# An FFT mixing layer and a hardswish MLP: the last inverse-transform stage packed into even and odd parts, mirrored output rows sent through a scratch tensor, and another ending of the last block

## The chip, the core and the metric

The kernel runs on one NeuronCore of a Trainium2 chip. TensorE (PE) multiplies matrices; its weight loads are shown as PEld. VectorE (DVE), ScalarE (ACT) and GpSimd (POOL) do elementwise work, and SyncE (SP) mostly issues DMAs. Each engine runs its own queue in order and waits for the others through semaphores. The metric is the device time of one execution in microseconds (us); the program's time is the median of several executions.

## The reference

```python
batch, seq, dim = (8, 3008, 256)          # n_freq = 1505, d_ff = 2048
X = np.fft.rfft(x, axis=1)
Y = X * (filt_r + 1j * filt_i)[None, :, :]
y = np.fft.irfft(Y, n=x.shape[1], axis=1).astype(np.float32)
h = y.reshape(24064, 256) @ w_in          # 256 x 2048
g = h * np.clip(h + 3.0, 0.0, 6.0) / 6.0
out = (g @ w_out).astype(np.float32)      # 2048 x 256
```

Everything is float32. The two weight matrices arrive as 64-bit floats and are turned into 32-bit ones by bit operations on DVE in the first microseconds of the kernel.

## The kernel before

**The transform.** A sequence of 3008 is written as 47 x 64 (token n = a * 64 + c). For each batch, `a_unit` (L391) transforms over a, storing 24 frequency rows k of real and imaginary parts in the DRAM tensor `z_tmp`; `b_unit` (L438, L447) transforms over c, `f_unit` and `y_unit` multiply by the filter, `bi_unit` (L482) transforms back over c and `g_store` (L499, L502) writes `g_tmp`. The last stage is `n_unit` (L535), which goes from 24 frequencies k back to 47 values of a, for each of 32 columns j. Column j of the transform gives two sets of 47 tokens, those of c = j and of the mirrored c = 64 - j. `t4_load` (L525 for batch 0, L528 for the others) brings five columns at a time, a chunk, from `g_tmp` to the tile `t4` with four DMAs, one column in each slot: rows 0-23 and 32-55 hold real and imaginary parts of c = j, rows 64-87 and 96-119 those of 64 - j. For each half dh of the 256 channels and each column, one matmul takes 128 rows x 128 channels of `t4` as its weights and streams the 94 columns of `wai[:, j]` (2 x 47 tokens); ACT copies the 470 results to `xn` (L541), channels on partitions and tokens along the row. `xn` is a ring of three blocks of 512 tokens. A float32 matmul shows in the profile as two passes, each a weight load and a matmul, so `n_unit` makes 20 passes for a chunk and half.

**The MLP.** 47 blocks of 512 tokens go through 8 steps p of 256 hidden columns each. Both products are done with a seven-multiplication scheme on 2 x 2 blocks (Strassen-Winograd). `t_sums` (L574) forms four sums of `xn` on POOL. `up_1` to `up_5` (L581) do seven 256-column matmuls into two PSUM tiles `al` and `be`; between them ACT and DVE copy partial sums out (L592, L593, L602, L607, L612, L621), and a later product into `al` may start only when the copy before it is done. `relu` (L626) and `hswish` (L631) give `g`; `g_sums` (L638-641) makes the sums for the down product, `down` (L657) does fourteen 128-column matmuls, and `out_1` to `out_5` (L693-716) add the seven results together into `o`. Block 0 alone is done without that scheme (`plain_up` L668, `plain_down` L679). `w_sums` (L308) turns the converted weights into the scheme's sums on POOL in steps 6 to 13.

**The order of work** is written out by hand. Step i of the main loop does the up product of (k, p) and the down product of the step before; `plan` holds, for each step, the units of the transform of the coming batch that are put after `up_1` (`do(True)`: matmul units) or at the end of the step (`do(False)`: the rest). The plan of `n_unit` is in `N_AT` and `N_FIRST`, and `t4_load` of a chunk is issued one chunk ahead, or for a batch's first chunk three steps ahead.

**The output.** `store` (L734) writes a finished block to `out` with one DMA for each run of up to 47 tokens within 128 partitions, 15 of them on average, all on SP's queue. After the last step, five DVE adds finish block 46 and its stores go out in runs of at most 32 rows over three queues.

Of the kernel before, what the change touches and what calls it, by code (L numbers as in the profile page):

```python
# [26 lines left out]
N = 3008  # L27
# [7 lines left out]
B = 8  # L35
# [16 lines left out]
RING = 3 * BLK  # L52
ND = (NJ + 1) * TOK


def outer(j, h):

    return (NC - j if j else HC) if h else j


def _make_tables():
# [3 lines left out]
    wai = np.zeros((P, HC, TOK))  # L65
# [26 lines left out]
    for q in range(64):  # L92
# [3 lines left out]
        wi[q, 3], wi[HALF + q, 3] = ab, sign * ab  # L96

        at = g % 2 * 32 + (q // 2 if q < 32 else 16 + (q - 32) // 2)
        wi[at, 0], wi[HALF + at, 0] = ab, sign * ab
# [11 lines left out]
        wi[q, 1], wi[HALF + q, 1] = ab, -ab  # L111
        wi[q, 2], wi[HALF + q, 2] = sign * ab, sign * ab
    start[:, :P] = np.eye(P)
    for j in range(HC):
        for h in range(2):
            to = slice(h * NA, (h + 1) * NA)
            for k in range(KH):
                m = 2.0 if k else 1.0
                th = 2 * np.pi * ((a * k * NC + outer(j, h) * k) % N) / N
                cs, sn = m * np.cos(th), m * np.sin(th)  # L120
                s = -1.0 if h else 1.0
                if j:
                    wai[k, j, to], wai[32 + k, j, to] = cs, -sn
                    wai[64 + k, j, to], wai[96 + k, j, to] = -s * sn, -s * cs
                else:
                    wai[h * 64 + k, j, to], wai[h * 64 + 32 + k, j, to] = cs, -sn
    direct = np.zeros((P, TC, ND))
    n = np.array([i * NC + outer(j, h) for j in range(NJ + 1) for h in range(2) for i in range(NA)])
    for k in range(KH - TC, KH):
        for q in range(64):  # L130
            th = 2 * np.pi * (((k + NA * q if q < 32 else NA * (q - 31) - k) * n) % N) / N
            direct[q, k - KH + TC], direct[HALF + q, k - KH + TC] = 2 / N * np.cos(th), -2 / N * np.sin(th)
    f = np.float32
    return wa.astype(f), (wai / N).astype(f), wb.astype(f), wi.astype(f), wf.astype(f), start.astype(f), direct.astype(f)
# [3 lines left out]
def kernel(  # L138
# [22 lines left out]
    g0_d = nc.dram_tensor("g0_tmp", (NC, 2, KH, D), FP32, kind="Internal").ap()  # L161
    g_d = nc.dram_tensor("g_tmp", (B, NU, 2, 2, NC, D), FP32, kind="Internal").ap()
# [22 lines left out]
    wai = const.tile([P, HC, TOK], FP32, name="wai")  # L185
# [3 lines left out]
    t4 = const.tile([P, 2 * NJ, D], FP32, name="t4")  # L189
    xn = const.tile([P, 2, RING], FP32, name="xn")  # L190
    w_all = const.tile([P, NP, 2, 7, P], FP32, name="w_all")
    w_in, w_out = ([w_all[:, p, i, :, :] for p in range(NP)] for i in range(2))
    half_c = const.tile([P, 1], FP32, name="half_c")
# [61 lines left out]
    def w_load(i, q):  # L255
        if W_AT[i] == "g":
            t = gp.tile([P, 7, 256], FP32, name="g")
            st["rest"] = t[:, 4:7, :].rearrange("p a n -> p (a n)")
            t = t.bitcast(I32)[:, 0:4, :].rearrange("p a n -> p (a n)")
        elif W_AT[i] == "x":  # L260
            t = xtp.tile([P, 4, 256], FP32, name="xt").bitcast(I32).rearrange("p a n -> p (a n)")
        else:
            t = op.tile([P, 1024], I32, name="bits", tag="o")
        q.dma_start(t.rearrange("p (a d) -> p a d", a=2), w_part(i)[0])
        st["bits", i] = t
# [39 lines left out]
    def w_sums(i, late):  # L305
        w = (w_in, w_out)[i % 2][i // 2]
        for o, x0, x1, op_ in (IN_SUMS, OUT_SUMS)[i % 2][3 * late:3 + late]:
            nc.gpsimd.tensor_tensor(out=w[:, o, :], in0=w[:, x0, :], in1=w[:, x1, :], op=op_)  # L308

# [9 lines left out]
    A11, S3, A12, A22, S1, S2, S4 = range(7)  # L319
    IN_SUMS = ((4, 1, 3, ALU.add), (5, 4, 0, ALU.subtract), (6, 2, 5, ALU.subtract), (1, 0, 1, ALU.subtract))  # L320
# [24 lines left out]
    def zt(dh):  # L345
        return (xn.rearrange("p a n -> p (a n)"), xs.rearrange("p i j d -> p (i j d)"))[dh]
# [141 lines left out]
    def g0_first(i):  # L488
        t = st["t3", 0, i]
        for v in range(2):  # L490
            for h in range(2):
                (nc.scalar, nc.sync)[v].dma_start(g0_d[ds(h * HC, NJ + 1), :, ds(2 * (i + v), 2), :].rearrange("c ri u d -> c ri (u d)"),
                                    t[ds(v * 64 + h * HC, NJ + 1)].rearrange("p ri u d -> p ri (u d)"))

    def g_store(b, i):
        t = st.pop(("t3", b, i))
        for v in range(2):
            if b == 0:
                nc.gpsimd.dma_start(g0_d[:, :, ds(2 * (i + v), 2), :].rearrange("c ri u d -> c ri (u d)"),  # L499
                                    t[ts(v, 64)].rearrange("p ri u d -> p ri (u d)"))  # L500
                continue
            nc.gpsimd.dma_start(g_d[b, i + v].rearrange("ri u c d -> c (ri u) d"), t[ts(v, 64)].rearrange("p ri u d -> p (ri u) d"))  # L502
# [3 lines left out]
    chunks = []  # L506
    for b in range(B):
        j = 0
        while j < HC:
            n = 1 if b == 0 and j == NJ else min(NJ, HC - j)  # L510
            chunks.append((b, j, n))
            j += n

    def token(i):
        b, j, n = chunks[i]
        return b * N + j * TOK, n * TOK

    def t4_load(i, k0=0, k1=KH, more=0):
        b, j, n = chunks[i]
        n += more  # L520
        for h in range(2):
            for ri in range(2):
                p0 = h * 64 + ri * 32
                if b == 0:
                    nc.sync.dma_start(t4[p0 + k0:p0 + k1, ds(i % 2 * NJ, n), :],  # L525
# [509 lines left out]
```

## Time and profile before

| | us |
|---|---|
| median of 3 runs | 2694.93 (2693.86 to 2696.06) |
| the profiled execution | 2693.65 |
| its span, first to last instruction | 2691.9 |

Mean granted TensorE clock: 0.998 of full speed.

| stretch of the span, us | PE busy | PEld busy | DVE | ACT | POOL | share of the DMA engines |
|---|---|---|---|---|---|---|
| 0 to 64, batch 0's transform | 57.55 | 40.57 | 48.24 | 25.45 | 15.62 | 0.88 |
| 64 to 128, block 0 | 62.61 | 38.59 | 58.89 | 26.51 | 8.89 | 0.79 |
| 128 to 170 | 41.34 | 36.52 | 25.78 | 20.18 | 31.53 | 0.49 |
| 694 to 1028, one batch in the middle | 334.00 | 297.12 | 254.38 | 164.80 | 44.86 | 0.24 |
| 2366 to 2676, no transform left but the last chunks | 310.00 | 292.61 | 204.03 | 153.45 | 18.74 | 0.06 |
| 2676 to 2692, the end | 3.89 | 3.51 | 4.96 | 1.35 | 4.11 | 0.12 |

Busy time is a union over the instructions of an engine. PE is busy without a gap from about 170 us to 2676 us; what it does there adds up to the time. [...]what one pass costs in a stream is the distance from start to start.

### The profile page before, as it was taken

The page shows a single profiled execution, that of the slowest core. Times are in us where ns is not written, and L with a number is a line of the kernel's source. Part 1 is how long each engine was busy: PE and PEld are TensorE (multiplying, and loading weights), DVE is VectorE, ACT ScalarE, POOL GpSimd, SP SyncE. Part 2 cuts the span into 40 slices and gives each one's busy share as a digit, 9 for nine tenths or more (in the row PEclk, how much of TensorE's full clock was granted, in tenths as well). Part 3 has the DMA queues.
Part 4 walks back from the last instruction along what each step waited for, and adds up shares of the span by engine and source line. Part 5 has one row for each costly group of instructions (what it writes and reads, how often), then busy time and mean ns, then how long its engine had stood idle before and what let it go on. Part 6 is the DMA issues. An engine that isn't in the chain of part 4 may idle for free.

```text
span 2691.9 us, 48842 instructions
## 1 busy us (share of the span) xinstructions
PE 2670.5 (99%) x18836; PEld 2364.3 (88%) x18836; DVE 2022.3 (75%) x3505; ACT 1306.9 (49%) x2612; POOL 369.4 (14%) x598
## 2 busy tenths in 40 slices
PE   9999999999999999999999999999999999999998
PEld 6688888888888889888898888888888898899997
DVE  7878867877678776787767777677876878766665
ACT  3444444545445454454544545445444454545443
POOL 2241021011210112101121101211012111000000
PEclk9999999999999999999999999999999999999999
DMA  8732233112331113311133212331123321110000
GB/s 254 213 90 66 53 97 98 55 37 54 90 96 55 38 53 89 96 55 39 53 89 96 56 40 55 89 93 56 39 57 90 93 62 31 42 31 18 18 9 17
DMA packets 106333, 185.95 MB, mean 69 GB/s; under 512 B 23333, under 2 KB 66021, under 8 KB 105781
## 3 DMA queue, kind: packets, MB, share of 16 engines
q1 hardware_dynamic: 88343, 138.12, 18.3%
q0 software_dynamic: 17152, 44.22, 6.2%
q8 instruction: 149, 2.44, 0.4%
q14 instruction: 83, 0.68, 0.1%
q10 hardware_dynamic: 606, 0.49, 0.1%
HBM read 110.80 MB, written 71.93 MB: 68 GB/s over the span
## 4 chain that ended last, share of the span: by engine, by line
PE 97%; DMA 1%; DVE 1%; ACT 0%; issue 0%; POOL 0%; SPq 0%; POOLq 0%; DVEq 0%; ACTq 0%
PE po L657 43%; PE al L581 24%; PE be L581 18%; PE psn L535 4%; PE psf L391 2%; PE psf L482 2%; PE psf L438 1%; PE po L679 1%; DMA g_tmp<-t 1%; PE al L668 0%; PE be L668 0%; DMA w_all<-in_x_dram 0%; PE psf L447 0%; PE po L447 0%; PE po L358 0%
## 5 line engine op out<-in xcount | busy, mean ns | idle before, releaser
L657 PEld LDWEIGHTS po<-w_all,g 128*128 128x128 f32 x10304 | 1363.2, 191 | 149.5 <-issue 41.4
L657 PE MATMUL po<-w_all,g 128*128 128x128 f32 x10304 | 1403.2, 276 | 0.6 <-DVE g L631 0.6
L626 ACT ACTIVATE r<-h,half_c 128x512 f32<-128x512 f32 x736 | 531.2, 722 | 329.6 <-DVE h L607 317.6
L631 DVE SCALAR_TENSOR_TENSOR g<-r,h 128x512 f32<-128x512 f32 x736 | 508.1, 690 | 205.3 <-ACT r L626 191.1
L581 PE MATMUL al<-xt,w_all 128*128 128x256 f32 x2208 | 660.1, 381 | 0.7 <-DVE h L612 0.6
L581 PE MATMUL be<-xn,w_all 128*128 128x256 f32 x1472 | 437.8, 379 | 0.0
L607 DVE TENSOR_TENSOR h<-be,s 128x512 f32<-128x512 f32 x368 | 254.3, 691 | 215.3 <-PE be L581 210.3
L581 PEld LDWEIGHTS al<-xt,w_all 128*128 128x128 f32 x2208 | 335.2, 192 | 2.1 <-DVE h L612 1.2
L581 PEld LDWEIGHTS be<-xn,w_all 128*128 128x128 f32 x1472 | 279.7, 190 | 37.9
L621 ACT ACTIVATE h<-al 128x256 f32<-128x256 f32 x368 | 141.3, 384 | 343.2 <-PE al L581 343.2
L612 DVE TENSOR_TENSOR h<-al,s 128x256 f32<-128x256 f32 x368 | 156.2, 425 | 165.8 <-PE al L581 164.8
L639 DVE TENSOR_TENSOR g<-g 128x512 f32<-128x512 f32 x368 | 256.2, 696 | 12.6
L602 ACT ACTIVATE s<-al 128x256 f32<-128x256 f32 x368 | 141.4, 384 | 205.9 <-PE al L581 203.8
L593 ACT ACTIVATE s<-be 128x256 f32<-128x256 f32 x368 | 141.4, 384 | 176.3 <-PE be L581 176.3
L581 PE MATMUL al<-xn,w_all 128*128 128x256 f32 x736 | 219.9, 381 | 0.5 <-ACT h L621 0.5
L581 PE MATMUL be<-xt,w_all 128*128 128x256 f32 x736 | 218.9, 379 | 0.0
L641 DVE TENSOR_TENSOR g<-g 128x256 f32<-128x256 f32 x368 | 170.1, 462 | 12.5
L592 ACT ACTIVATE s<-al 128x256 f32<-128x256 f32 x368 | 141.4, 384 | 70.3 <-PE al L581 70.3
L638 DVE TENSOR_TENSOR g<-g 128x256 f32<-128x256 f32 x368 | 157.3, 428 | 12.6
L581 PEld LDWEIGHTS be<-xt,w_all 128*128 128x128 f32 x736 | 139.8, 190 | 18.9
L412 POOL DMA_DIRECT2D z_tmp<-t x192 | 95.6, 505 | 417.3 <-DVE t L405 399.0
L502 POOL DMA_DIRECT2D g_tmp<-t x84 | 52.9, 634 | 581.9 <-ACT t L485 581.9
(144 smaller groups left out, 1810.2 us busy)
## 6 DMA issues: line engine op xcount, KB each, us to landing
g_tmp<-t POOLq DMA_DIRECT2D x96, 256.0 KB, 3.7
t<-g_tmp SPq DMA_DIRECT2D x188, 120.0 KB
t<-z_tmp SPq DMA_DIRECT2D x42, 512.0 KB
z_tmp<-t POOLq DMA_DIRECT2D x192, 96.0 KB, 3.3
out_dram<-o SPq DMA_DIRECT2D x321, 47.0 KB
xs<-in_x_dram SPq DMA_DIRECT2D x112, 128.0 KB
ft<-in_filt_r_dram SPq DMA_DIRECT2D x168, 64.0 KB
ft<-in_filt_i_dram SPq DMA_DIRECT2D x168, 64.0 KB
```

The source lines that it names most:

```text
L581: nc.tensor.matmul(ps, w_in[p][:, w, :], x, start=start, stop=stop, skip_group_check=True)
L592: nc.scalar.activation(out=s[:, 0, :], in_=al, func=AXT.Copy)
L593: nc.scalar.activation(out=s5, in_=be[:, 1, :], func=AXT.Copy)
L602: nc.scalar.activation(out=s[:, 1, :], in_=al, func=AXT.Copy)
L607: nc.vector.tensor_tensor(out=st["h"][0].rearrange("p (a n) -> p a n", a=2), in0=be, in1=s, op=ALU.add)
L612: nc.vector.tensor_tensor(out=st["h"][1][:, 256:512], in0=al, in1=s5, op=ALU.add)
L626: nc.scalar.activation(out=r, in_=st["h"][i], func=AXT.Relu, bias=half_c, scale=1.0 / 6.0)
L631: nc.vector.scalar_tensor_tensor(out=st["g", k, p][:, o:o + 2, :].rearrange("p a n -> p (a n)"), in0=st["r", i], scalar=1.0, in1=st["h"][i ...
L638: v.tensor_tensor(out=g[:, G1, :], in0=g[:, G3, :], in1=g[:, G22, :], op=ALU.add)
L639: v.tensor_tensor(out=g[:, G3:G2 + 1:2, :], in0=g[:, G3:G1 + 1, :], in1=g[:, G11:G11 + 1, :].broadcast_to([P, 2, 256]), op=ALU.subtract)
L641: v.tensor_tensor(out=g[:, G4, :], in0=g[:, G12, :], in1=g[:, G2, :], op=ALU.subtract)
L657: nc.tensor.matmul(st["po", k][bank][:, part, u, :], g[:, a, ts(u, P)], w_out[p][:, w, :], start=(p == 0 and n in OPENS and u == 0), stop= ...
```

## The change

**Even and odd parts.** For a real sequence, the tokens of c = j and their mirror images are C + S and C - S, where C comes from the real parts (cosines) and S from the imaginary parts (sines) of `g_tmp` alone. `bi_unit`'s table `wi` is changed so that its outputs are already these sums and differences. A column needs 48 rows for C and 48 for S. `t4_load` packs five columns' 240 rows into two weight tiles of 128 and 112 rows, for C and for S, and `n_unit` streams a table `groups` of 3 x 47 = 141 columns past each: four matmuls for a chunk and half in place of five. The third column's 48 rows lie partly in one tile and partly in the other, and both add into its 47 results. Columns left over (0 and 1, and seven columns of the last batch) are done one by one with 94 table columns and 96 rows. There are 46 full chunks and 20 single columns in the kernel, apart from the six columns that `direct` and `n_first` do at the start.

`xn` now holds C and S, 256 of each for a block, and the combination is moved into the sums of the MLP's scheme: `t_sums` makes seven POOL operations where there were four, and the weights' sums are others, with two of the seven scaled by 2 and -2 on ACT after POOL has made them.

**Stores.** Half 0 of a block's tokens goes to `out` directly, half 1 (the mirrored rows) to the DRAM scratch `o_tmp` in one DMA; when 16 columns are complete (15, 9, 10, 6 or part of one at the edges), one DMA from DRAM to DRAM copies them to their rows of `out`, backwards.

**The last block.** Its columns are arranged so that 7 DMAs write each half of it, its last down step is done without the seven-product scheme into two free PSUM tiles, and the outputs of the steps before it are added beside that. The column `b12` of the last weights, which the scheme overwrites, is saved and put back for this.

```diff
-RING = 3 * BLK
+PAIRS = BLK // 2
+RING = 3 * PAIRS
...
-    t4 = const.tile([P, 2 * NJ, D], FP32, name="t4")
-    xn = const.tile([P, 2, RING], FP32, name="xn")
+    t4 = const.tile([P, 8, D], FP32, name="t4")
+    xn = const.tile([P, 2, 2, RING], FP32, name="xn")
...
     def w_sums(i, late):
         w = (w_in, w_out)[i % 2][i // 2]
+        if late and i == 2 * NP - 1:
+            nc.scalar.activation(out=b12, in_=w[:, 1, :], func=AXT.Copy)
         for o, x0, x1, op_ in (IN_SUMS, OUT_SUMS)[i % 2][3 * late:3 + late]:
             nc.gpsimd.tensor_tensor(out=w[:, o, :], in0=w[:, x0, :], in1=w[:, x1, :], op=op_)
+        if late and i % 2 == 0:
+            for o, scale in ((S1, 2.0), (A22, -2.0)):
+                nc.scalar.activation(out=w[:, o, :], in_=w[:, o, :], func=AXT.Copy, scale=scale)
...
+    def t4_load(i):
...
+        both = t4[:, ds(s0, 4), :].rearrange("p (c s) d -> p s c d", c=2)
+        for q, j in enumerate(js):
+            for hh in range(2):
+                r, k = q * ATOM + hh * KH, 0
+                while k < KH:
+                    s_, p0 = divmod(r + k, P)
+                    m = min(KH - k, P - p0)
+                    nc.sync.dma_start(both[p0:p0 + m, s_, :, :],
+                                      g_d[b, hh * HC + j, :, k:k + m, :].rearrange("ri k d -> k ri d"))
+                    k += m
...
     def n_unit(i, dh):
         ps = psF.tile([P, 512], FP32, name="psn", tag="f")
-        for q in range(chunks[i][2]):
-            nc.tensor.matmul(ps[:, ts(q, TOK)], t4[:, i % 2 * NJ + q, ts(dh, P)], wai[:, chunks[i][1] + q, :], start=True, stop=True)
...
+        if len(js) == NJ:
+            for c in range(2):
+                for s_ in range(2):
+                    r = ROWS[s_]
+                    nc.tensor.matmul(ps[:, ds(c * NJ * NA + s_ * 2 * NA, SPAN)], t4[0:r, s0 + 2 * c + s_, ts(dh, P)],
+                                     groups[0:r, (js[-1] - 2) // NJ, s_, :], start=c == 0 and s_ == 0, stop=True,
+                                     skip_group_check=True)
+            pieces = [(0, n, o, ps[:, 0:2 * n])]
+        else:
+            for q, j in enumerate(js):
+                w = edges[0:2 * ATOM, FIRST.index(j), :] if i >= TAIL and j else ones[0:2 * ATOM, j, :]
+                nc.tensor.matmul(ps[:, ts(q, TOK)], t4[0:2 * ATOM, s0 + q, ts(dh, P)], w, start=True, stop=True)
...
     def t_sums(k):
-        for o, x0, x1 in ((0, b12, b11), (1, b22, t[:, 0, :]), (2, b22, b12), (3, b21, t[:, 1, :])):
-            nc.gpsimd.tensor_tensor(out=t[:, o, :], in0=x0, in1=x1, op=ALU.subtract)
+        for o, x0, x1, op_ in ((f1, c0, s0, ALU.subtract), (u, c0, c1, ALU.add), (v, s0, s1, ALU.add),
+                               (f4, u, v, ALU.subtract), (f5, u, v, ALU.add), (f2, c1, s1, ALU.add), (f3, f1, f2, ALU.add)):
+            nc.gpsimd.tensor_tensor(out=o, in0=x0, in1=x1, op=op_)
...
+    def last_down():
+        p, v, add = NP - 1, nc.vector.tensor_tensor, ALU.add
+        g, o = st["g", LAST, p], st["o", LAST][0]
+        hswish(LAST, p, 1)
+        ps = [psF.tile([P, 512], FP32, name="psf", tag="f") for t in range(2)]
+        for i, a in ((0, G11), (1, G12)):
+            for t in range(2):
+                for u in range(2):
+                    nc.tensor.matmul(ps[t][:, ts(u, D)], g[:, a + t, ts(u, P)],
+                                     w_out[p][:, 2 * i:2 * i + 2, :].rearrange("p j m -> p (j m)"),
+                                     start=i == 0 and u == 0, stop=i == 1, skip_group_check=True)
+        out_4(LAST)
+        v(out=o_at(LAST, 0, 1), in0=st["po", LAST][3][:, 1, :, :], in1=o_at(LAST, 0, 1), op=add)
+        for t, qs in ((0, (nc.sync, nc.gpsimd, nc.scalar)), (1, (nc.sync, nc.scalar))):
+            both = o[:, t, :, :].rearrange("p u d -> p (u d)")
+            v(out=both, in0=ps[t], in1=both, op=add)
+            store_last(t, qs)
...
+    def store(k):
+        o = st["o", k][0]
+        nc.sync.dma_start(o_d[ds(k * PAIRS, PAIRS)].rearrange("(u p) d -> p u d", p=P), o[:, 1, :, :])
+        for u, p, m, b_, j, a in runs(k):
+            for h in range(1 if j else 2):
+                nc.sync.dma_start(raw(out, b_ * N + row(j, h, a), [[NC * D, m], [1, D]]), o[p:p + m, h, u, :])
+        for b_, r, j, m, na in BACK.get(k, ()):
...
+            nc.sync.dma_start(bass.AP(tensor=out.tensor, offset=to, ap=a0),
+                              bass.AP(tensor=o_d.tensor, offset=o_d.offset + r * D, ap=a1))
+
+    def store_last(h, qs):
...
+        for n, (p, m, u, nu, to, du) in enumerate(parts):
+            ap = [[NC * D, m], [du, nu], [1, D]]
+            qs[n % len(qs)].dma_start(bass.AP(tensor=out.tensor, offset=out.offset + to, ap=ap), o[p:p + m, h, u:u + nu, :])
...
-            if up:
-                up_1(k, p)
+            if not up:
+                last_down()
+                break
+            up_1(k, p)
+            ends = k == LAST and p == NP - 1
...
-        v(out=o_at(k, 1, 1), in0=po[2][:, 0, :, :], in1=o_at(k, 1, 0), op=add)
-        v(out=o_at(k, 1, 0), in0=st["o", k][1][:, 1, :, :], in1=o_at(k, 1, 0), op=add)
-        store(k, 2, 4, qs)
-        v(out=o_at(k, 0, 1), in0=po[2][:, 0, :, :], in1=o_at(k, 0, 1), op=add)
-        v(out=o_at(k, 0, 1), in0=po[3][:, 1, :, :], in1=o_at(k, 0, 1), op=add)
-        store(k, 0, 2, qs)
```

In the step marked `ends`, `out_1`, `out_2` and `out_3` of block 46 run already beside the products of the step before the last. The last two chunks (`TO`) are written to `xn` in eight pieces for each half dh, because their tokens are laid out for `store_last`. The table for the first six columns is loaded at the start into a part of `wai` (564 columns, where eight columns' 752 were loaded before), the rest (1880 columns, before 2256) in step 0, and the first part again for the last batch near the end.

## The prediction

> **What bounds the kernel.** I read the page's busy times first, then the chain that ended last.
>
> ```profile
> PE 2670.5 (99%) x18836; PEld 2364.3 (88%) x18836; DVE 2022.3 (75%) x3505; ACT 1306.9 (49%) x2612; POOL 369.4 (14%) x598
> ...
> PE 97%; DMA 1%; DVE 1%; ACT 0%; issue 0%; POOL 0%; SPq 0%; POOLq 0%; DVEq 0%; ACTq 0%
> ```
>
> PE carries 97% of the chain. In the trace's waits, the rows in which PE waits for another engine add up to 3.2 us between 64 us and 2680 us. So a microsecond taken from PE's stream comes off the time, and what other engines gain or lose counts only where it makes PE wait, or after PE's last instruction.
>
> Next the price of one PE pass. The timeline of PE alone, around one `n_unit` with both halves (columns: start us, extent us, engine, line, form, count); a count in the last column divides the distance to the next start:
>
> ```profile
> 2023.32 0.59 PE L581 MATMUL be<-xt,w_all 128*128 128x256 f32 x2
> 2023.75 0.59 PE L581 MATMUL be<-xn,w_all 128*128 128x256 f32 x2
> 2024.18 2.37 PE L535 MATMUL psn<-wai,t 128*128 128x94 f32 x20
> 2026.38 0.64 PE L657 MATMUL po<-w_all,g 128*128 128x128 f32 x4
> ...
> 2027.72 1.05 PE L657 MATMUL po<-w_all,g 128*128 128x128 f32 x8
> 2028.62 0.38 PE L581 MATMUL al<-xt,w_all 128*128 128x256 f32 x1
> ```
>
> 256 columns: 0.43 / 2 = 0.215 us a pass. 128 columns: (2028.62 - 2027.72) / 8 = 0.1125. 94 columns: (2026.38 - 2024.18) / 20 = 0.110. From 256 to 128 columns the price halves; from 128 to 94 it hardly falls. Below 128 columns the pass is held by something that isn't the streamed columns, and each pass has its weight load beside it. This is where the change works: 94-column passes waste stream.
>
> **The last transform stage.** Before: the page counts 1000 passes at L535 (43, 24, 18% of the chain are the MLP, 4% this stage), 1000 x 0.110 = 110.0 us. After: 46 full chunks x 2 halves x 4 matmuls x 2 passes = 736 passes of 141 columns, and 20 single columns x 2 x 2 = 80 of 94 columns; the six first columns (24 passes elsewhere) don't change. No row has 141 columns. A straight line between 128 and 256 columns gives 0.1125 + 13/128 x 0.1025 = 0.123. The slope of the wide rows alone (the 512-column L668: four passes in 1.72 us in the chain, 0.43 each; 0.43 / 512 = 0.00084 a column) gives 0.118. I take 0.121, between them. 736 x 0.121 + 80 x 0.110 = 97.9, so **-12.1 us**; with 0.118 it is -14.4, with 0.123 -10.7. The early `plain_down` passes of 256 columns (L679) take 3.65 us for 16 in the chain, 0.228, 0.013 over the others; were the new passes to carry that too (0.136), -1.1 would be left. That is the outer end.
>
> A rule speaks against this. The Trainium skill (TensorE: Matmul & The Clock Gate, "Back-to-back issue gap") prices a pass by its columns, N / 2.4 + 2.5 ns, and Perfetto Trace Analysis ("Engine Utilization") halves the rate for float32, so about N / 1.2 + 2.5: 80.8 ns for 94 columns, 120 for 141. The stage would then go from 80.8 to 736 x 0.120 + 80 x 0.0808 = 94.8 us, 14 us dearer, because the change streams 111,296 columns where there were 94,000. The row decides: 110 ns, not 81, for 94 columns. The same page's "LDWEIGHTS" has 128 / 1.2 = 107 ns for loading 128 weight columns, whatever the rows, which fits the floor. For 141 columns the rule's 120 agrees with my 0.121.
>
> **The end.** Timeline from PE's last work to the last store:
>
> ```profile
> 2675.45 1.50 PE L657 MATMUL po<-w_all,g 128*128 128x128 f32 x12
> 2676.82 0.69 DVE L631 SCALAR_TENSOR_TENSOR g<-r,h 128x512 f32<-128x512 f32 x1 [1.47 <-ACT r L626]
> 2677.56 2.94 PE L657 MATMUL po<-w_all,g 128*128 128x128 f32 x24 [0.62 <-DVE g L631]
> ...
> 2682.57 0.42 DVE L1003 TENSOR_TENSOR o<-po,o 128x256 f32<-128x256 f32 x1
> 2682.22 4.73 SPq L734 DMA_DIRECT2D out_dram<-o  x10
> ```
>
> Before, PE waits 0.62 us for the second `hswish`, runs 24 passes, DVE then does six adds up to 2682.99, and SP issues until 2686.95 (10 DMAs, 0.47 each). After, the eight passes of `down(7, 3)` of the step before end at 2676.34 and the first half of the plain product (8 passes x 0.217 = 1.74) needs only the first `hswish`, done at 2675.34: PE no longer waits. The second half starts at 2678.08 (its `hswish` slips by 0.15 behind `out_3`, to 2677.64) and ends at 2679.8. `out_4` and one more add (3 x 0.42, POOL's 0.73 beside) end by 2678.95, under PE. Then 0.69 us on DVE for half 0 (ready 2679.2, done 2679.95) and 0.69 for half 1 (done 2680.75). SP issues three DMAs of half 0 and four of half 1 from 2680.0: 7 x 0.47 = 3.3, to 2683.3 in place of 2686.95. The same 512 KB has to land in a shorter time, so I count **-3.3 us** (-4.2 to -2.3). Stall gone, the late one next is SP's issuing.
>
> **The scaling copies on ACT.** New, sixteen of 128 x 128, about 0.25 us each (the 128x94 copy at L565 takes 0.249). They sit at the end of steps 6 to 13 and wait for POOL's sums, and behind them on ACT stand the next step's `relu` and the copies that release `al`. POOL, from the timeline:
>
> ```profile
> 122.48 25.16 POOL L308 TENSOR_TENSOR w_all<-w_all 128x128 f32<-128x128 f32 x43 [20.39 <-DVE w_all L302]
> ```
>
> 0.585 us a sum, starting at 122.48. Step 6's copies need the sixth, 126.0; ACT stands from 118.3 to 126.0 where it would have run `relu` at 122.04. PE's next need is the tile `al` at 128.23, and `relu` plus `hswish` end at 127.9: covered. Step 7's copies need the fourteenth sum, 130.7; the copy of `al` (128.86 before) ends at 131.35, and `up_2` moves from 130.64 to 131.4: +0.8. The delayed DVE conversions stay under `plain_down` (3.5 us). In step 11 the sums stand behind the longer `t_sums`, ACT stalls 1.2 us, and `up_2` at 163.83 just gets its copy. **+1.0 us**, 0 to +4.
>
> **The rest, with its cover.** `t_sums` grows from 4 to 7 operations (3 x 0.73 = 2.2 us, 45 times), under POOL's 86% idle; the first block user comes at least one step (6.15 us) later; uncovered it would cost 2.2 us a block. Behind it in POOL's queue stand `z_tmp` stores, for which ACT waits only two units later. A chunk's load goes from 4 DMAs to 11 on SP. By the sources' durations, the old pattern issues in 0.749 and the one of batch 0, which the new one resembles, in about 0.37-0.43:
>
> ```profile
> L528 SPq DMA_DIRECT2D t<-g_tmp x196: 744/749/1919, 344.1 to 2504.3; - x196
> L525 SPq DMA_DIRECT2D t<-g_tmp x32: 265/369/1129, 49.2 to 221.7; - x32
> ```
>
> So 11 x 0.43 = 4.7 for 4 x 0.79 = 3.2. A store has 1 + 7 DMAs for 15, and 18 times in the kernel a copy that waits behind it for the scratch write to land (3.3 us for a POOL store); SP is then held about as long as the 14 us it is now. In step 0 the two chunks put 22 DMAs before the weight loads at 81.09 and 81.83, which slip by some 6 us; they are first used at 91.5: just covered, 0 to +2. The first evictions gain two small ones (0.2 us, under PE's first matmul). The last two chunks' eight pieces of about 0.19 us delay `al`'s copy by 0.6 us, with slack of about 0.6: **+0.5** for four places (0 to 1.5).
>
> **Sum**: -12.1 - 3.3 + 1.0 + 0.5 = **-13.9 us**, against the profiled execution 2693.65 - 13.9 = 2679.75 (span 2678.0); its 1.28 us under the median carried over, **2681.0 us**.
>
> **Rivals.** (1) *The wide passes cost 0.136*, as in `plain_down`'s early rows: -1.1 - 3.3 + 1.5 = -2.9, **2692**. For it: 64-128 us shows that 256 columns can cost 6% more. Against: that was at a DMA share of 0.79; in the middle (0.24) every row is at 0.215. 7%. (2) *The ACT waits land on PE in all eight steps*, 1.5 us each: -12.1 - 3.3 + 12 + 0.5, **2692**. Against: from step 8 on POOL is ahead of ACT. 5%. (3) *SP's queue becomes the bound for the loads; slower*: a scratch copy (1.5 MB read and written, about 6 us at 250 GB/s) or slower issues (11 x 0.79 = 8.7) put a batch's first chunk behind its `n_unit`. In the fourth batch that load is issued by 1012.2 and used at 1020.9; landing takes 2.8 to 6.0, so about 3 to 6 us are free. Each microsecond beyond counts in full, because `n_unit` stands ahead of `down` in PE's order. It decides from 2.3 us on each of six first chunks; at 4 us, +24: **2705**. Against: the copies leave at a block's first step, the first chunk's load 20 us later, the others a block ahead. 6%. That the passes don't fall to 816 is excluded by the loops.
>
> **Chances.** Forecast 80%, 2676 to 2688; (1) 7%, (2) 5%, (3) 6%, something else cheaper or dearer 2%. Range **2676 to 2690**: low with 0.118 and the tail's better end, high with half of the gain of the stage lost. A measurement here tells about 0.2%, 5.4 us, from no change, so faster means below 2689.5: 0.84, same 0.10 (rivals 1 and 2 and the forecast's edge), slower 0.06.
>
> **What would show it.** L535's line as 816 passes, the stage's 16 passes spanning 1.9 to 2.0 us where 20 spanned 2.2; PE idle between 128 and 134 us of about 1 us more; SP's last issue near 3.6 us earlier against PE's last matmul; no PE wait on a `t<-g_tmp` DMA. It is wrong if the 141-column passes are spaced by over 0.13 us, or if PE waits for `t4` or the copies on ACT more than 3 us in all.

## The result and the profile after

The changed kernel takes **2680.57 us** (median of 4 executions, 2680.14 to 2681.81), the kernel before 2695.0 us (4 executions, 2693.86 to 2696.06). The ratio is 0.9948, with a 95% interval of 0.9935 to 0.9960: 14.4 us faster; 2681.0 us had been predicted. The profiled execution of the changed kernel took 2680.88 us, span 2679.1, against 2693.65 and 2691.9 before. So the profiles compare with 12.8 us; the other 1.6 us of the medians is that the profiled execution of before was 1.3 under its median and this one 0.3 over.

The page of the changed kernel, busy times and shares of the chain:

```profile
PE 2661.1 (99%) x18640; PEld 2351.6 (88%) x18640; DVE 2069.1 (77%) x3503; ACT 1311.9 (49%) x2672; POOL 493.0 (18%) x731
...
PE 94%; DVE 3%; DMA 2%; POOL 0%; issue 0%; ACT 0%; SPq 0%; POOLq 0%; DVEq 0%; ACTq 0%
```

PE is still the bound. POOL has gained 124 us of busy time and DVE 47, although DVE has two instructions fewer: its instructions have become longer (last section).

**The stage.** PE's timeline around the same `n_unit` as before (start us, extent us, engine, line, form, count):

```profile
2020.20 2.10 PE L625 MATMUL psn<-wai,t 128*128 128x141 f32 x16
2022.14 0.61 PE L766 MATMUL po<-w_all,g 128*128 128x128 f32 x4
```

These are both halves dh of a chunk, 8 passes for each, where there were 10 for each (not 20 for each, as the description of the kernel before has it). From start to the next start the 16 passes take 1.94 us, 0.121 each; they overlap, for the profile gives a single one 0.283 us. 20 had taken 2.20. The trace counts 736 passes of 141 columns, half of them with 128 rows and half with 112, and 80 of 94 columns.

**The end.** The timeline from `up_5`'s matmul to the last stores:

```profile
2668.09 0.60 PE L690 MATMUL al<-xn,w_all 128*128 128x256 f32 x2
...
2672.93 3.24 SPq L890 DMA_DIRECT2D out_dram<-o  x7
...
2673.19 1.02 POOL L890 DMA_DIRECT2D out_dram<-o  x2 [1.36 <-DVE o L785]
```

From `up_5`'s start to the end of the span 11.01 us pass (2679.1 - 2668.09). Before it was 16.89 (2691.9 - 2675.01): **-5.9 us**, with no wait of PE left in it. The row of before is

```profile
2675.01 0.60 PE L581 MATMUL al<-xt,w_all 128*128 128x256 f32 x2
```

The distance repeats well: it is 16.8 to 16.9 us in all five profiles with the old ending and 11.0 to 11.1 in all five with the new one.

**The scaling copies.** ACT's and PE's timeline between steps 6 and 9 (in brackets the idle time ahead, and what ended it):

```profile
127.12 0.31 ACT L369 ACTIVATE w_all<-w_all 128x128 f32<-128x128 f32 x1 [7.85 <-POOL w_all L366]
...
128.41 0.67 ACT L735 ACTIVATE r<-al,half_c 128x512 f32<-128x512 f32 x1
...
129.94 0.67 PE L690 MATMUL al<-xt,w_all 128*128 128x256 f32 x2 [0.61 <-DVE g L740]
...
132.56 0.31 ACT L369 ACTIVATE w_all<-w_all 128x128 f32<-128x128 f32 x1 [1.15 <-POOL w_all L366]
...
133.20 0.70 PE L690 MATMUL al<-xt,w_all 128*128 128x256 f32 x2 [0.59 <-ACT s L701]
```

ACT stands for 7.85 us until POOL has made the sums; only then the `relu` of step 7 runs (128.41), and PE waits at 129.94 for the `hswish` behind it. The second pair of copies, done at 132.87, holds the copy of `al` (L701) behind it, and PE waits again at 133.20.

**Where the time went.** The starts of the stage's passes (`n_unit`) are landmarks that both profiles share. The fourth column is what the wider passes alone would have made of each stretch (0.26 us where 20 passes become 16, 0.13 where 10 become 8):

| stretch between landmarks, us before | before | after | less the stage's gain | over it |
|---|---|---|---|---|
| start to 60.75 (first passes of the stage) | 60.75 | 61.92 | 60.75 | +1.2 |
| 60.75 to 97.43 | 36.68 | 36.51 | 36.55 | 0.0 |
| 97.43 to 258.20 (ACT's copies, block 1) | 160.77 | 163.32 | 159.85 | +3.5 |
| 258.20 to 352.47 | 94.27 | 94.68 | 94.01 | +0.7 |
| 352.47 to `up_5` of the last block | 2322.54 | 2311.66 | 2311.7 | -0.1 |
| `up_5` of the last block to the end | 16.89 | 11.01 | 16.89 | -5.9 |

With the stage's -12.1 (46 x 0.264) the sum is -12.7, against -12.8 between the spans.

### The profile page after: what moved, and what is told of

It reads as the page before. It is cut to its first block, busy times and chain, and to the rows that moved or that the text cites. A ratio compares the mean times of both kernels' runs of the same rounds, so it can differ in the third digit from the quotient of the medians.

```text
span 2679.1 us, 48744 instructions
## 1 busy us (share of the span) xinstructions
PE 2661.1 (99%) x18640; PEld 2351.6 (88%) x18640; DVE 2069.1 (77%) x3503; ACT 1311.9 (49%) x2672; POOL 493.0 (18%) x731
## 4 chain that ended last, share of the span: by engine, by line
PE 94%; DVE 3%; DMA 2%; POOL 0%; issue 0%; ACT 0%; SPq 0%; POOLq 0%; DVEq 0%; ACTq 0%
PE po L766 43%; PE al L690 23%; PE be L690 17%; PE psn L625 3%; PE psf L543 2%; PE psf L452 2%; PE psf L499 1%; DVE g L740 1%; DMA g_tmp<-t 0%; DMA ft<-in_filt_i_dram 0%; DVE y L337 0%; DVE w_all L358 0%; DVE y L355 0%; PE psn L632 0%; DMA wa<-wb_t 0%
## 5 line engine op out<-in xcount | busy, mean ns | idle before, releaser
L740 DVE SCALAR_TENSOR_TENSOR g<-r,h 128x512 f32<-128x512 f32 x736 | 530.5, 721 | 198.0 <-ACT r L735 184.5
L690 PE MATMUL be<-xt,w_all 128*128 128x256 f32 x1472 | 437.8, 379 | 0.0
L690 PEld LDWEIGHTS be<-xt,w_all 128*128 128x128 f32 x1472 | 279.7, 190 | 37.9
L686 POOL TENSOR_TENSOR xt<-xn 128x256 f32<-128x256 f32 x184 | 153.8, 847 | 661.7 <-ACT xn L641 633.2
L690 PE MATMUL be<-xn,w_all 128*128 128x256 f32 x736 | 219.0, 379 | 0.0
L750 DVE TENSOR_TENSOR g<-g 128x256 f32<-128x256 f32 x367 | 175.3, 478 | 12.5
L701 ACT ACTIVATE s<-al 128x256 f32<-128x256 f32 x368 | 141.2, 384 | 67.0 <-PE al L690 67.0
L747 DVE TENSOR_TENSOR g<-g 128x256 f32<-128x256 f32 x367 | 157.5, 429 | 12.5
L690 PEld LDWEIGHTS be<-xn,w_all 128*128 128x128 f32 x736 | 139.8, 190 | 19.1 <-DVE g L740 0.2
```

The costliest lines, as they stand in the source:

```text
L686: nc.gpsimd.tensor_tensor(out=o, in0=x0, in1=x1, op=op_)
L690: nc.tensor.matmul(ps, w_in[p][:, w, :], x, start=start, stop=stop, skip_group_check=True)
L740: nc.vector.scalar_tensor_tensor(out=st["g", k, p][:, o:o + 2, :].rearrange("p a n -> p (a n)"), in0=st["r", i], scalar=1.0, in1=st["h"][i ...
L747: v.tensor_tensor(out=g[:, G1, :], in0=g[:, G3, :], in1=g[:, G22, :], op=ALU.add)
L750: v.tensor_tensor(out=g[:, G4, :], in0=g[:, G12, :], in1=g[:, G2, :], op=ALU.subtract)
```

## Experiments

All twelve are compared with the kernel before, run on the same chip beside them (median 2694.3 to 2694.9 us); those built on the changed kernel are also set against its 2680.57. Differences of 1 to 3 us lie inside the intervals of the totals, so the smaller ones are read as distances in the profiles.

### What a pass below 128 columns costs

```diff
 # b_wide128
-    nc.tensor.matmul(ps[:, ts(q, TOK)], t4[...], wai[:, chunks[i][1] + q, :], start=True, stop=True)
+    nc.tensor.matmul(ps[:, ds(q * TOK, n)], t4[...],
+                     wai.rearrange("p j n -> p (j n)")[:, ds(j * TOK, n)], start=True, stop=True)   # n = 128
 # b_half_rows
+    for v in range(2):
+        nc.tensor.matmul(ps[:, ds(q * TOK + v * NA, NA)], t4[...], wai[:, j, ts(v, NA)], start=True, stop=True)
 # b_half_weights
+    for v in range(2):
+        nc.tensor.matmul(ps[ts(v, 64), ts(q, TOK)], t4[:, slot, ds(dh * P + v * 64, 64)], wai[:, j, :], start=True, stop=True)
```

> The kernel before, with 984 of the 1000 passes of its last transform stage streaming 128 columns in place of 94; the further 34 columns are overwritten or never read. Theory (a pass of up to 128 columns is held by something other than its columns): 0.1125 us in place of 0.110, so +2.5 us, and 20 passes span 2.25 us. Rival (a pass costs its columns): by the rule of N/1.2 + 2.5 ns 28 ns more for each pass, +28 us; by 0.110 x 128/94, +39 us.

> The kernel before, with each 94-column pass of the last transform stage cut into two of 47 columns with the same weights; the output stays the same. Theory (each pass pays a floor whatever its columns): 2000 passes at 0.110 us in place of 1000, +110 us. Rival (a pass costs its columns): the same columns in all, so 0 to +2.5 us.

> The kernel before, with each pass of the last transform stage cut into two with half of the weight columns (64 in place of 128), each streaming the 94 columns. Theory (the floor is the load of 128 weight columns): with half of the load the pass falls to what 94 columns cost by the slope of the wide passes, 94 x 0.00084 = 0.079 us, 2000 x 0.079 = 158 us in place of 110, +48 us. Rival (the floor is a fixed cost of each pass, whatever its weights): 2000 x 0.110, +110 us.

| kernel | time | ratio to before, 95% interval |
|---|---|---|
| b_wide128 | 2694.45 | 1.0001 (0.9993 to 1.0009) |
| b_half_rows | 2814.17 | 1.0444 (1.0425 to 1.0464) |
| b_half_weights | 2694.66 | 1.0001 (0.9992 to 1.0011) |

The timeline of PE in b_wide128, with 20 passes of 128 columns, and in b_half_rows, with 20 of 47:

```profile
2026.96 0.59 PE L584 MATMUL be<-xn,w_all 128*128 128x256 f32 x2
2027.39 2.39 PE L537 MATMUL psn<-wai,t 128*128 128x128 f32 x20
...
2030.07 0.60 PE L584 MATMUL al<-xt,w_all 128*128 128x256 f32 x2
```

```profile
396.22 0.59 PE L583 MATMUL be<-xn,w_all 128*128 128x256 f32 x2
396.65 2.33 PE L536 MATMUL psn<-wai,t 128*128 128x47 f32 x20
...
399.33 0.60 PE L583 MATMUL al<-xt,w_all 128*128 128x256 f32 x2
```

In b_wide128 968 passes have 128 columns; 32, those of the last column, keep their 94. To leave out where the profile puts the edge between two forms, take the distance from the group ahead to the second group behind. With 20 passes of 94 columns it is 3.11 us in the kernel before; with 20 of 128 it is 3.11 as well (2030.07 - 2026.96), with 20 of 47 also 3.11 (399.33 - 396.22). **A pass costs 0.111 us at 47, 94 and 128 columns alike.** Even the 2.5 us that the theory had for 128 columns aren't there. The kernel of halved passes is 120 us slower (119.9 between the medians, 117.6 between the spans) for 1000 more passes; 111 of it are these, 1.4 lie at the front, and the last 5 us weren't followed up. As the price of a pass in a stream, pricing by columns is refuted on both sides.

What paces the passes can be read from the starts that the trace keeps for each pass and each weight load. In the 91 groups of each of these kernels the second pass follows the first after 0.041, 0.081 and 0.109 us at 47, 94 and 128 columns (two groups of b_wide128 excepted), which is near the columns at the wide rows' 0.00084 us each. Only the later passes are 0.111 to 0.112 apart. The weight loads run on another beat: the first one starts 0.21 us ahead of its pass, under the wide pass before the group, the second as the first pass starts, and from there they follow one another in steps of 0.110 to 0.112 us, whatever the columns. So the passes fall into step with the loads, not the loads with the passes. In the changed kernel, with 141 columns, the first distance is 0.120 us and the later ones 0.121: there the columns take longer than the load.

With half of the weight columns neither forecast came out: no change, where +48 and +110 had been expected. Its timeline:

```profile
2024.12 0.59 PE L583 MATMUL be<-xn,w_all 128*128 128x256 f32 x2
2024.64 1.84 PE L536 MATMUL psn<-wai,t 128*64 128x94 f32 x40
...
2026.97 0.60 PE L583 MATMUL al<-xt,w_all 128*128 128x256 f32 x2
```

The same distance is 2.85 us with 40 such passes, 2.04 with 20 and 1.55 with 8. That is 0.0405 us a pass, 0.081 for the pair that does the work of one 94-column pass, and 0.34 us more for each group. 1000 x (0.111 - 0.081) = 30 us are gained and 91 x 0.34 = 31 us lost at the groups' edges, so the total stands still. A fixed price of a pass is refuted: twice the passes cost no more. Both forecasts had the two halves run one after the other. The trace has them side by side: the passes start in pairs, 0.006 to 0.008 us apart within a pair and about 0.08 from pair to pair. A pair's 0.081 is about what 94 columns cost by the wide rows' slope (0.079), so the floor of 0.111 is gone with the loads of 128 weight columns. What the 0.34 us at the edges are stays open.

### ACT's scaling copies, moved to where ACT is idle

```diff
-        if late and i % 2 == 0:        # end of w_sums, steps 6 to 13
-            for o, scale in ((S1, 2.0), (A22, -2.0)):
-                nc.scalar.activation(out=w[:, o, :], in_=w[:, o, :], func=AXT.Copy, scale=scale)
+        at(NP - 1, w_scale, 0)         # the first weight: step 7
...
                 up_4(k, p)
+            if k == 1 and p < NP - 1:
+                w_scale(p + 1)         # the same two copies, behind relu(0)
```

> The changed kernel with its sixteen scaling copies on ACT moved from the end of steps 6 to 13, where they wait for POOL's sums, into the gap behind relu(0) of the next step (those of the first weight to the end of step 7). Theory (the copies' waits hold ACT and cost PE about 3.2 us): PE's distance from the start of plain step 7 (121.06) to up_2 of step 12 (167.45) falls from 46.4 to about 43.2 us, and the time from 2680.6 to about 2677.5. Rival (the loss there is that of POOL's longer t_sums or of the longer loads): the distance stays at 46.4 and the time within 0.5 us of 2680.6.

Time 2678.99 us, ratio 0.9941 (0.9928 to 0.9953). From plain step 7 (120.51) to `up_2` of step 12 (164.41) 43.9 us pass in place of 46.4; from the pass group at 97.89 to that at 258.61 it is 160.7 in place of 163.3. **-2.5 to -2.6 us** of the 3.2 expected. `relu` of step 7 now runs at 122.43, and the first copies find their sums made:

```profile
127.88 0.31 ACT L370 ACTIVATE w_all<-w_all 128x128 f32<-128x128 f32 x1
128.41 0.31 ACT L370 ACTIVATE w_all<-w_all 128x128 f32<-128x128 f32 x1 [0.22 <-POOL w_all L366]
```

So the copies' waits are the cause of 2.6 of the 3.5 us in this stretch; 0.9 stays with the change and wasn't taken apart (PE still waits 0.51 us there for a sum that POOL makes). The version is the fastest one measured, but the interval of its time reaches into that of the changed kernel; what shows the gain is the profile.

### What the end hangs on

```diff
 # a_no_pool_stores, a_three_queues (the latter with the copies moved as above)
-        for t, qs in ((0, (nc.sync, nc.gpsimd, nc.scalar)), (1, (nc.sync, nc.scalar))):
+        for t, qs in ((0, (nc.sync, nc.scalar)), (1, (nc.sync, nc.scalar))):
+        for t, qs in ((0, (nc.sync, nc.gpsimd, nc.scalar)), (1, (nc.scalar, nc.gpsimd, nc.sync))):
 # b_no_pool_stores
-        po, qs = st["po", k], (nc.sync, nc.scalar, nc.gpsimd)
+        po, qs = st["po", k], (nc.sync, nc.scalar)
 # a_old_last_step: last_down()
-        # plain product: 16 passes of 256 columns, then one add for each half
+        g_sums(k, NP - 1)
+        down(k, NP - 1, 1); down(k, NP - 1, 2, 4); out_1(k); down(k, NP - 1, 5, 6); out_2(k)
+        down(k, NP - 1, 7, 3); out_3(k)
+        # the four adds of before, store_last(1, ...) behind the second, store_last(0, ...) behind the fourth
```

> The changed kernel with the last block's fourteen stores on the queues of SP and ACT alone (SP issues 8 in place of 7, POOL none in place of 2). Theory (what follows SP's last issue, 4.95 us before and 2.93 after the change, hangs on the stores of POOL's queue): the stretch from SP's last issue to the end falls below 2.9 us and the time is 2680 or less. Rival (it hangs on the landing of the last stores, whatever their queue): the stretch stays at 2.9 us, SP's one further issue adds 0.47 us, time 2681.0.

> The changed kernel with the last down step as it was before (28 passes of 128 columns and six adds of the seven products, in place of 8 of 256 columns and fewer adds behind PE), but with the few stores of the change. Theory (the plain step and the few stores each bring a part of the 5.9 us by which the stretch from up_5's last start to the end became shorter): the last sum ends 7.98 us behind that start as before, in place of 5.74, so +2.2 us, 2682.8. Rivals: the few stores bring all of it (0, 2680.6); the plain step brings all of it (+5.9, 2686.5).

> The kernel before with its last 26 stores on the queues of SP and ACT alone (13 each in place of 10, 8 and 8 on POOL). Theory (the 4.95 us from SP's last issue to the end hang on the eight stores of POOL's queue): the stretch falls to about 2.9 us, SP's three further issues add 1.4 us, so -0.6 us, 2693.7. Rival (the stretch is that of the last landing on any queue): it stays at 4.95 us, +1.4 us, 2695.7.

> The changed kernel with the scaling copies moved as in the kernel above, and the stores of the last half dealt to ACT, POOL and SP in turn (SP issues 5 in place of 7, ACT 5, POOL 4 in place of 2). Theory (the end follows the last issue on any queue by some 2.9 us): SP's last issue comes 0.8 us earlier, time 2678.2 against 2679.0. Rival (POOL's stores end later than those of the other queues, as in the kernel before): the stretch from up_5's last start to the end grows above 11.0 us by up to 1.5.

The chain that ended last in the kernel before closes with POOL's stores and POOL's queue:

```profile
2684.03 2.06 POOL out_dram L734 x4
2686.09 0.51 POOLq L1030
```

All distances in us, from the timeline of each profile; "issue" is the end of a queue's last store issue:

| kernel | time | `up_5` to end | POOL's last issue to end | SP's last issue to end |
|---|---|---|---|---|
| before | 2695.0 | 16.89 | 5.30 | 4.95 |
| b_no_pool_stores | 2693.25 | 15.31 | none | 2.23 |
| after | 2680.57 | 11.01 | 4.89 | 2.93 |
| a_scale_moved | 2678.99 | 11.01 | 4.87 | 3.04 |
| a_three_queues | 2680.84 | 12.26 | 5.08 | 5.40 |
| a_old_last_step | 2682.63 | 13.07 | 4.83 | 3.00 |
| a_no_pool_stores | 2681.95 | 12.00 | none | 3.70 |

In every profile in which POOL stores, the span ends 4.8 to 5.3 us behind POOL's last issue, while the distance from SP's last issue runs from 2.9 to 5.4. The timeline of a_three_queues is the plainest case:

```profile
2672.88 2.02 SPq L891 DMA_DIRECT2D out_dram<-o  x5
2672.88 2.29 ACTq L891 DMA_DIRECT2D out_dram<-o  x5
2673.14 2.08 POOL L891 DMA_DIRECT2D out_dram<-o  x4 [1.36 <-DVE o L786]
```

SP's last issue is over at 2674.90, 6.86 us behind `up_5`'s start where a_scale_moved, on which this kernel is built, has 7.97, and yet the end comes 1.25 us later, because POOL issues until 2675.22. The theory ("some 2.9 us behind the last issue on any queue") falls, its rival stands. In b_no_pool_stores, with 14 stores on SP and 12 on ACT, SP issues 1.1 us longer and ACT 1.6, and the end still comes 1.6 us sooner (0.6 expected): the theory had the cause, and its size was too small.

What makes POOL's queue the late one stands in the engines' closing instructions, which the trace keeps and the timeline leaves out. In the kernel before, the last store of any queue has landed at 2688.91 and SP is through with its waits for the stores at 2689.36; but POOL closes with a DRAIN that is over only at 2691.09, 4.49 us behind POOL's last issue, and 0.77 us later the span ends. In the changed kernel this DRAIN is over at 2678.22, 4.00 us behind the last issue, SP at 2677.67; in a_three_queues at 2679.39, SP at 2678.01. So POOL's stores do not land late; its DRAIN ends 4.0 to 4.5 us behind its last issue, in every profile in which POOL stores.

In the changed kernel POOL issues its two stores first and is done at 2674.21; there the DRAIN ends only 0.55 us behind SP, so little was to be gained, and taking POOL's stores away cost 1.0 us. Both cases expected for a_no_pool_stores (a stretch below 2.9 us, or 2.9 as before) were wrong: without stores on POOL its DRAIN is over at 2675.80, SP's own waits count, until 2679.42, and the stretch is 3.70. In b_no_pool_stores it is 2.23. Of these 1.5 us, 1.0 is the landing: the last store has landed 2.00 us behind SP's last issue in the first, 0.98 in the second. Why it takes longer stays open; the stores of the first are up to 64 KB, those of the second up to 32 KB.

With the last down step as before, the distance is 13.07: **+2.06 us**, 2.2 expected, and PE's wait of 0.62 us is back. This kernel also takes back that `out_1` to `out_3` ran a step early. So the new arithmetic of the ending brings 2.1 of the 5.9 us, and what is left for the fewer stores is 3.8.

### The other queues' work: SP and POOL

```diff
 # a_direct_stores: store(k)
-        nc.sync.dma_start(o_d[ds(k * PAIRS, PAIRS)]..., o[:, 1, :, :])
         for u, p, m, b_, j, a in runs(k):
-            for h in range(1 if j else 2):
+            for h in range(2):
...
-        for b_, r, j, m, na in BACK.get(k, ()):   # copies out of the scratch
 # a_loads_doubled: t4_load(i)
-                    nc.sync.dma_start(both[p0:p0 + m, s_, :, :], g_d[b, hh * HC + j, :, k:k + m, :]...)
+                    for c in range(2):
+                        nc.sync.dma_start(both[p0:p0 + m, s_, c, :], g_d[b, hh * HC + j, c, k:k + m, :])
 # b_pool7: t_sums(k)
-        for o, x0, x1 in ((0, b12, b11), (1, b22, t[:, 0, :]), (2, b22, b12), (3, b21, t[:, 1, :])):
+        for o, x0, x1 in (..., (0, b12, b11), (2, b22, b12), (3, b21, t[:, 1, :])):
```

> The changed kernel with the mirrored half stored straight from its tile: two stores for each run of rows in place of one, no write to the scratch and no copies out of it. The rows of that half are written in ascending order, so they land in each other's places. Theory (SP's queue and the scratch lie beside PE's work): 0, within 0.5 us of 2680.6. Rival (the copies that wait for the scratch write hold SP, and loads come late for it): up to 2 us faster, with fewer PE waits.

> The changed kernel with each DMA of a five-column chunk's load cut into two (22 in place of 11 for a chunk, the same bytes): 4.7 us more on SP for a chunk. Theory (the prediction's cover: 3 to 6 us are free at the first chunk of each of six batches, and each microsecond beyond counts in full): 0 to 1.7 us for each of the six, 0 to +10 us, with PE waits on t<-g_tmp. Rival (the loads have much more room than that): under +1 us and no such waits behind 64 us.

> The kernel before, with three of its four sums of each block on POOL made a second time (7 operations in place of 4, same results): 46 x 3 = 138 operations more on POOL. Theory (POOL's operations slow DVE's that read both operands from SBUF, and this costs PE about 0.7 us around 254 to 292 us): time +0.7 us, DVE's mean of g<-r,h up from 0.690 to about 0.72 us and its total by 30 to 50 us. Rival (the new slowness of DVE is that of other parts of the change): DVE's means and the time unchanged.

> The changed kernel as it is, run again beside the others. Theory (the 1.1 us by which it was behind at 65 us is the DMA timing of one execution, since the kernel before with wider passes was 2.8 us behind there and with more sums on POOL 0.1 us ahead): its first passes of L663, which began at 61.92 us, begin somewhere between 60.6 and 63.5, and the time stays within 1 us of 2680.6. Rival (the change itself delays the front): they begin at 61.9 again.

**Direct stores** are slower, 2683.84 us, ratio to before 0.9962 (0.9948 to 0.9976); neither case had that. SP's timeline at the first block's store in the changed kernel, then with direct stores, and PE's wait in the latter:

```profile
140.89 6.08 SPq L873 DMA_DIRECT2D out_dram<-o  x7
147.07 5.76 SPq L473 DMA_DIRECT2D z_tmp<-t  x8
```

```profile
140.24 14.72 SPq L872 DMA_DIRECT2D out_dram<-o  x14
...
168.13 1.89 PE L508 MATMUL psf<-t,wf 128*128 128x256 f32 x4 [3.54 <-DMA t<-z_tmp]
```

SP takes 14.7 us for 14 stores in place of 6.1 for 7 and 0.4 for the write to the scratch, the stores to `z_tmp` behind them begin at 155.06 in place of 147.07, and PE waits 3.54 us for what is loaded back from there. Between 157 and 202 us the kernel falls 4.4 us behind the changed one, and nowhere else. So the way by the scratch isn't idle bookkeeping: one write and half of the stores make the room on SP that the longer loads take.

**Doubled loads** cost 10.6 us (2691.12, ratio 0.9987, 0.9979 to 0.9995). The size is what the theory allowed, the place is not. The list of PE's waits begins with

```profile
PE psf L452 <- DMA xs<-in_x_dram: 6.8, 1, 6.8
```

which is one wait at 107.85, and between the pass groups of 98.43 and 148.97 the kernel loses 10.9 us; the 4.1 beside the wait weren't taken apart. At the first chunks of the six later batches it loses nothing: behind 160 us its lag only goes from 12.4 to 12.8. In step 0 SP issues 44 DMAs in a row where the changed kernel has 22 (22.5 us against 12.4), and the load of `x` for the next batch stands behind them. The cover that the prediction worried about is wide where it looked, in the middle, and used up in the first steps.

**More sums on POOL** in the kernel before: 2695.72 us, ratio 1.0006 (0.9997 to 1.0014), which alone settles nothing. In the profile the stretch from 258.20 to 352.47 us grows from 94.27 to 95.35 (+1.1), the rest stands still, and DVE's operations change as they do in the changed kernel. The line's answer for one of them (shortest, median, longest in ns), before and with more sums:

```profile
L471 DVE TENSOR_TENSOR y<-s x84: 689/689/690, 181.6 to 2316.3; 64x512 f32<-64x512 f32 x84
```

```profile
L471 DVE TENSOR_TENSOR y<-s x84: 689/689/1108, 181.7 to 2317.4; 64x512 f32<-64x512 f32 x84
```

The mean of `g<-r,h` goes from 690 to 710 ns (720 expected, 721 in the changed kernel), its total by 14.5 us and DVE's by 36.8 (30 to 50 expected). Of DVE's 47 us more in the changed kernel this and `y<-s` (687 to 810 ns, 2 x 84) account for most. So POOL's operations do it; whether all of the 0.7 us between 258 and 352 is theirs isn't certain, since 0.34 us of the 1.1 here is a wait for an `x` load.

**The changed kernel again**: 2681.43 us, ratio 0.9950 (0.9938 to 0.9963). Its first passes of the stage begin at 61.64, which settles nothing between the two cases. Over the profiles of all kernels on either base, whose programs hardly differ up to there, they begin at 60.6, 60.7, 60.75, 61.1, 62.2 and 63.6 (before) and at 61.2, 61.4, 61.6, 61.9, 61.9, 62.2, 63.4 and 64.0 (after). The starts scatter over 3 us on either side, so 1.2 us between two executions proves nothing; the medians, 60.9 and 61.9, leave it open whether about 1 us of it belongs to the change.

## Why the prediction was right, step by step

- **PE is the bound, and a pass below 128 columns is held by something else than its columns.** Right, and shown: 0.111 us at 47, 94 and 128 columns. The weight load beside the pass, which the prediction named as fitting, is what paces it: the loads keep steps of 0.11 us where the passes' own first distances are 0.041 to 0.109, and with loads of 64 columns the floor is gone.
- **The stage: 0.121 us for 141 columns, -12.1 us.** Exact: 1.94 us for 16 passes, 46 x 0.264 = 12.1. The 0.121 was taken between two ways of reading the rows, 0.118 and 0.123; that it fell on the measured value to the last digit is in part luck. The rule weighed there, 120 ns for 141 columns and 81 for 94, does not speak against the change. The first distances in the groups, 41, 81, 109 and 120 ns at 47, 94, 128 and 141 columns, are what it gives as an estimate (41.7, 80.8, 109.2 and 120); it only leaves out the weight loads. The Trainium skill (TensorE: Matmul & The Clock Gate, "Back-to-back issue gap") says as much: the formula is for an isolated matmul and counts too little at small N, because in a stream of weight loads and matmuls both set the spacing. Rival 1 (0.136) is excluded by the spacing.
- **The end: -3.3 us.** Right in direction, too small: -5.9. PE's and DVE's part was exact: the last sum ends 5.74 us behind `up_5`'s start, as computed. The mis-sized term is the stretch behind SP's last issue, which the sum carried over unchanged at 4.95 us. SP's issue did come 3.9 us earlier relative to `up_5` (11.94 to 8.08 us; 3.65 predicted), but what the end hung on was POOL's DRAIN behind its last issue. That issue came 5.5 us earlier, 2.4 because the data were ready sooner and 3.1 because it issues two stores in place of eight. The chain that ended last in the kernel before, which closes with POOL's stores, could have told it.
- **ACT's scaling copies: +1.0 us, 0 to +4.** The mechanism was right, the size not: about +2.6, shown by moving them. Two steps failed. `relu` of step 7 was to end its chain at 127.9 behind copies done at 126.0; POOL's sums started at 125.16 in place of 122.48, the copies held ACT until 128.41, and PE waited 0.61 us. And `up_2` of step 12, which "just gets its copy", waited 0.84 for a copy of `al`. The wait at step 8's `up_2` was foreseen (+0.8, measured 0.59 in brackets). Rival 2, the waits in all eight steps, did not occur.
- **Two late chunks in small pieces: +0.5 us.** They cost nothing visible: the stretch from 352 us on is 0.1 us off without them.
- **`t_sums`, hidden under POOL's idle time.** Right for POOL's own time. That POOL's operations lengthen DVE's wasn't thought of; it costs PE up to 0.7 us.
- **Loads, stores and scratch copies on SP: covered, 0 to +2 in step 0.** In the middle the cover is wide: no PE wait on `t<-g_tmp` behind 64 us, and twice the DMAs don't change that. Rival 3 (2705) is refuted there. What the estimate of 0.43 us for an issue missed is the first steps, where 22 take 12.4 us, 0.56 each; the margin held (0.0 us lost from 60.75 to 97.43), but a second such row costs 10.9 us.

The profiled sum was to be -13.9 and is -12.8: the tail gave 2.6 more, the copies and their neighbourhood took 2.5 more, the front and the stretch from 258 us took 1.9 that no step had, and the pieces gave back 0.5 (0.2 is left over from rounding and the stretches near zero). So the misses, 3.1 us one way and 4.4 the other, largely cancel: that the total came so close to the forecast 2681.0 is in part luck, while the stage's term was right by itself.

## What to carry to other kernels

Price a matmul pass by distances between starts and look for the width below which it stops falling; columns added up to there are free, and fewer, wider passes pay. Ask of a program's end which queue its last event belongs to, and give the queue that finishes slowest the fewest and earliest stores. An instruction that waits for a slower engine is best placed where its input is ready and its own engine is idle anyway: the same sixteen copies cost 2.6 us more in one place than a few instructions later.

## What the runs showed of the hardware

POOL and DVE hold each other up. The timeline of the changed kernel:

```profile
261.14 0.69 DVE L531 TENSOR_TENSOR y<-s 64x512 f32<-64x512 f32 x1
...
267.86 0.70 DVE L740 SCALAR_TENSOR_TENSOR g<-r,h 128x512 f32<-128x512 f32 x1
267.96 1.18 POOL L686 TENSOR_TENSOR xt<-xn 128x256 f32<-128x256 f32 x1
268.59 1.10 DVE L531 TENSOR_TENSOR y<-s 64x512 f32<-64x512 f32 x1
269.22 1.05 POOL L686 TENSOR_TENSOR xt<-xt 128x256 f32<-128x256 f32 x1
```

Beside POOL's sums a DVE operation with both operands in SBUF takes 1.10 us in place of 0.69, and POOL's takes up to 1.18 where its mean in the kernel before is 0.75. DVE operations that read PSUM keep their times (the add of `be`, 691 ns before and 690 after). The Trainium skill ("SBUF — State Buffer", "Who interferes with whom") says that a DVE instruction with two SBUF inputs contends with a GpSimd instruction that reads SBUF, and these rows agree.

It also says that this contention is an exclusive lock, and that the order of issue decides who blocks. The rows agree with that too. DVE's `g<-r,h` starts first, at 267.86, and keeps its 0.70; POOL's sum, started at 267.96, ends 0.58 us behind it, at 269.14; DVE's `y<-s`, started at 268.59, ends 0.55 behind that, at 269.69; POOL's next ends 0.58 behind that, at 270.27. Each runs only when the other is done, so the extra time is waiting. Over the whole kernel, the 65 POOL sums during which such a DVE operation starts keep their 0.73 us, and the 50 `y<-s` that start while POOL runs take 1.10.
